# Two interleaved memory-transformer layers: Q, K and V in 128-row chunks with row-tiled tails, PSUM in single banks, W2 summed over two units

## The chip, the cores and the metric

The kernel runs on one core of one Trainium2 chip. The metric is the device time of one execution in microseconds, here as the median of 3 runs. TensorE (PE) multiplies, VectorE (DVE) and ScalarE (ACT) move results out of PSUM and do the elementwise work, GpSimd (POOL) does one small operation a normalization, and SyncE (SP) issues the loads of weights.

## The reference

Two blocks alternate, twice: a segment-recurrent attention A and a gated feed-forward B, each on the normalized input and with a residual.

```python
x = x + A(layernorm(x)); x = x + B(layernorm(x))
x = x + A(layernorm(x)); x = x + B(layernorm(x))   # the same weights both times
# A: S = 2048 in 64 segments of 32 rows, 8 memory rows, D = 576, 32 heads of 128
for s in range(64):
    h = concatenate([mem, x[32*s:32*s+32]])         # 40 rows
    q, k, v = h @ Wq, h @ Wk, h @ Wv                # each 576 -> 32 x 128
    p = softmax(where(mask, q @ k.T * 128**-0.5, -1e9))
    o = (p @ v) @ Wo                                # back to 576
    mem, out[s] = o[:8], o[8:]
# B: silu(x @ w1) * (x @ w3) @ w2, with 576 -> 4608 -> 576
```

All inputs and the output are bf16. A segment needs the memory that the segment before it left, so the 64 segments of a layer follow each other.

## The kernel before

The two layers run interleaved: at step t layer 0 works on segment t and layer 1 on segment t - 8 (`LAG = 8`), so 56 of the 72 steps hold both layers (80 columns) and the first and last eight hold one (40). Every four steps a job runs the FFN for one block of 128 rows of each layer; it is spread over the next four steps. It goes by 18 units (`NPR`) of 256 of the 4608 columns; a unit's w1, w3 and w2 are loaded anew for each job.

What runs in which order is decided before the program is built. `make_nodes` describes the work as nodes, each with an engine, an assumed duration, dependencies, a priority and the buffer slots that it takes and gives back. `plan` walks through them like a list scheduler, and the instructions are emitted in the order that comes out, which every engine's queue keeps. A node with the engine "AD" goes to ScalarE or VectorE, whichever is free first.

The steps of attention, by the names in the trace: QK (for 8 units of 4 heads, Q and K of those heads into PSUM, then copied to `QKT`), VX and VM (V of the segment's rows and of the memory rows, copied to the tiles `VX` and `VM`), and then for 4 groups of 8 heads: SC (scores into `SB`), softmax on VectorE with the exponential on ScalarE (`SME`, `STAT`, `PB`), TR (transposes of `PB`, copied to `PTS`), PV (copied to `OT`) and WO (summed in `YB` over all groups). At the end of a step the new memory is copied from `YB` into the columns of the next step's `HT`, the transposed normalized input ("Ymem"). In the FFN, FF is the product with w1 and w3 in one, `HTT` its gated activation, and W2 the way back, which VectorE adds to the residual `XR`.

D = 576 is 9 chunks of 64 rows. `HT` and `XTB` hold every chunk twice, once in each half of the 128 partitions, and the weights hold Wq (w1) in the upper half and Wk (w3) in the lower one, so that two 64-row matmuls run at a time. V's weights lie the same way, by heads, and V's outputs take column strips of 32, so that eight matmuls of 64 rows and 32 columns run at a time. The core of QK:

```python
for hl in range(4):
    for c in range(NCH):
        for r in (0, 1):
            rr = slice(r * R64, (r + 1) * R64)
            self.mm(self.pair(pair)[:, r, hl * 2 * QW + q0:hl * 2 * QW + q1], self.T.WQK[rr, c, h0:h0 + E],
                    HTt[rr, POS[c], q0:q1], c == 0, c == NCH - 1, tile_position=(r * R64, 0))
```

Each `mm` is a weight load and a matmul of its own. PSUM is 3 pairs of banks that all these products share, one bank for the scores and the transposed probabilities (`SB`), and one for `YB`. A pair comes free when both its halves have been copied out. Every instruction goes through a helper, so that in the profile all matmuls have line 467, VectorE's work line 473 and ScalarE's line 470; the tiles tell them apart.

Of the kernel before, what the change touches and what calls it, by code (L numbers as in the profile page):

```python
# [35 lines left out]
EW_LAT = 0.13  # L36
NOW = 1.0e18

# [8 lines left out]
class Node:  # L47
# [3 lines left out]
    def __init__(self, eng, dur, fn, deps=(), prio=0.0, mode=None, acq=(), rel=(), name="", lat=None):  # L51
# [4 lines left out]
        self.outs, self.ready, self.start, self.end, self.by = [], 0.0, None, None, None  # L56
        self.left = len(self.deps)


def plan(nodes, pools, mode_pen=0.12, hold=0.0):  # L60
# [29 lines left out]
    while done < len(nodes):  # L90
# [50 lines left out]
        for o in n.outs:  # L141
            lat = n.lat
            if o.eng == e and e in ("ACT", "DVE", "PE"):
# [10 lines left out]
def ew(n, psum=True):  # L154

    return (0.07 + n * 0.000833 if psum else 0.11 + n * 0.000833, 0.065 + n / 960.0)


def dve(n):
    return 0.065 + n / 960.0  # L160


def actc(n):
    return 0.07 + n * 0.000833


def make_nodes(em, nseg, dma_bw=230e3, load_bw=340e3):
# [4 lines left out]
    def node(*a, **k):  # L172
# [4 lines left out]
    pools = {"pair": 3, "s": 1, "y": 1, "qkt": 4, "vx0": 1, "vx1": 1, "vm": 1, "sme": 2, "pb0": 1, "pb1": 1, "pts": 1, "ot": 1,  # L177
             "xr": 4, "xn": 2, "w13": 2, "w2": 2, "htt": 2}
    nst = nseg + LAG

# [4 lines left out]
    def load(name, nbytes, prio, fn):  # L185
        return node("DMA", nbytes / load_bw, fn, prio=prio, name=name, lat=2.0)

    kb = lambda rows, cols: rows * cols * 2
    ld_x0, ld_m0 = None, None
# [3 lines left out]
    order = [("qk", 0), ("qk", 1), ("v", 0), ("v", 1), ("v", 4), ("v", 5), ("v", 2), ("v", 3), ("v", 6), ("v", 7),  # L193
             ("o", 0), ("qk", 2), ("qk", 3), ("o", 1), ("qk", 4), ("qk", 5), ("o", 2), ("qk", 6), ("qk", 7), ("o", 3)]
    for what, i in order:
# [3 lines left out]
        elif what == "v":  # L199
            ld_v[i] = load("ldv", kb(576, 512), pr, em.load_v(i))  # L200
        else:
            ld_o[i] = load("ldo", kb(1024, 576), pr, em.load_o(i))

    m0p = Slot("pair")
    m0t = node("PE", 0.3, em.m0_tr(m0p), deps=[ld_m0], prio=-5, mode="full", acq=[m0p], name="m0tr")
    m0e = node("DVE", 0.5, em.m0_ev(m0p), deps=[m0t], prio=-5, rel=[m0p], name="m0ev")

# [4 lines left out]
    stores = {}  # L212
# [3 lines left out]
    def ln_nodes(tag, src, xn, deps, prio, writers, wdeps):  # L216

        acq = [] if src is xn else [xn]
        a = node("DVE", 0.72 + 0.12 + 0.07, em.ln_stats(src, xn), deps=deps, prio=prio, acq=acq, name=tag + "stats")
        b = node("POOL", 0.45, em.ln_pow(xn), deps=[a], prio=prio, name=tag + "pow")  # L220
        c = node("DVE", 0.5, em.ln_norm(src, xn), deps=[b], prio=prio, name=tag + "norm")
        pair = Slot("pair", users=len(writers))
        d = node("PE", 5 * 0.056, em.ln_tr(xn, pair), deps=[c] + list(wdeps), prio=prio, mode="full", acq=[pair], rel=[xn],
                 name=tag + "tr")
        out = []
        for eng, n, fn in writers:
            cost = ew(n)
            out.append(node(eng, cost if eng == "AD" else (cost[0] if eng == "ACT" else cost[1]), fn(pair), deps=[d],
                            prio=prio, rel=[pair], name=tag + "wr"))
        return c, out  # L230

    def ht_writers(li, g):
        w = []
        for r in (0, 1):
            for half in (0, 1):
# [815 lines left out]
```

## Time and profile before

| | |
|---|---|
| Median of 3 runs | 3476.67 us (3463.12 to 3481.11) |
| The profiled execution: time, span of its instructions | 3458.9 us, 3456.9 us |
| PE busy | 2949.1 us (85%), 92853 matmuls |
| VectorE, ScalarE, GpSimd busy | 2242.8 us (65%), 1207.7 us (35%), 65.3 us (2%) |
| DMA | 327.62 MB, mean 95 GB/s |

Busy time is the union of an engine's instructions. A matmul's row begins when it starts and has a modelled end, and the next one can start long before that end, so that a mean of 199 ns for one matmul and a rate of many more than five a microsecond go together. Idle time is charged to what released the next instruction; "issue" is a wait for nothing that the profile shows.

### The profile page before, as it was taken

Reading aid. Unit: us, or ns where it says so; the run is one execution under the profiler, and the core shown is the slowest. Engines: PE = TensorE matmul, PEld = TensorE weight load, DVE = VectorE, ACT = ScalarE, POOL = GpSimd, SP = SyncE. Lnnn points to the kernel's source line nnn. Section 1 sums busy time; section 2 is a strip of 40 time slices with the busy share of each in tenths; the row PEclk is TensorE's granted clock in tenths of the full one; section 3 lists DMA queues with packets and bytes.
Section 4 is the critical chain, followed back from the end, with each engine's and each line's share of the span. In section 5 each row is a group of like instructions: output and inputs, shape, how many; then the busy total and the mean of one; then the engine's idle time right before and its main releaser. Section 6 shows DMA issues by size and latency. Waiting matters only on the chain.

```text
span 3456.9 us, 196772 instructions
## 1 busy us (share of the span) xinstructions
PE 2949.1 (85%) x92853; PEld 2414.3 (70%) x92853; DVE 2242.8 (65%) x4915; ACT 1207.7 (35%) x2607; POOL 65.3 (2%) x108
## 2 busy tenths in 40 slices
PE   3777888899888988889898988999888989888776
PEld 2566767777777777777777777777777777766664
DVE  2355657677666766676776766676766777666554
ACT  1233333343333334343433333343333334332221
POOL 0000000000000000000000000000000000000000
PEclk8789999999999999999999999999999999999898
DMA  9135444434343433434343443443343443444448
GB/s 223 28 71 107 91 106 91 96 80 92 76 108 77 97 90 81 96 82 92 80 101 80 98 92 75 96 100 78 79 98 80 102 89 80 96 91 96 94 107 192
DMA packets 485515, 327.62 MB, mean 95 GB/s; under 512 B 16344, under 2 KB 482144, under 8 KB 484704
## 3 DMA queue, kind: packets, MB, share of 16 engines
q1 hardware_dynamic: 481632, 307.96, 40.3%
q8 instruction: 725, 11.88, 1.5%
q0 software_dynamic: 3072, 7.08, 0.7%
q14 instruction: 86, 0.70, 0.1%
HBM read 310.26 MB, written 2.36 MB: 90 GB/s over the span
## 4 chain that ended last, share of the span: by engine, by line
PE 63%; DVE 17%; issue 11%; ACT 5%; SPq 2%; DMA 1%; POOL 0%; POOLq 0%; ACTq 0%; DVEq 0%
PE pair L467 51%; PE YB L467 7%; PE SB L467 5%; DVE HTT L473 4%; DVE STAT L473 3%; DVE PB L473 3%; DVE SME L473 3%; SPq L476 2%; DVE XR L473 1%; ACT HT L470 1%; ACT SME L470 1%; DMA W<-in_B_w_dram 1%; DVE VX L473 1%; DVE HT L473 1%; DVE LNS L473 1%
## 5 line engine op out<-in xcount | busy, mean ns | idle before, releaser
L467 PE MATMUL pair<-HT,WQK 64*128 64x80 bf16 (+1 forms) x41472 | 812.7, 195 | 265.9 <-issue 226.1
L467 PEld LDWEIGHTS <-WQK 64*128 64x128 bf16 x42048 | 771.6, 97 | 337.2 <-issue 307.2
L467 PE MATMUL pair<-XTB,W 64*128 64x256 bf16 (+1 forms) x11016 | 610.0, 262 | 30.2 <-issue 11.4
L467 PEld LDWEIGHTS <-W 64*128 64x128 bf16 x11016 | 505.1, 95 | 89.5 <-issue 44.8
L470 ACT ACTIVATE QKT<-pair 128x320 bf16<-128x320 f32 (+1 forms) x790 | 301.4, 407 | 735.9 <-PE pair L467 703.2
L467 PE MATMUL pair<-WV,HT 64*32 64x512 bf16 (+1 forms) x14400 | 453.0, 390 | 52.8 <-DVE HT L473 15.4
L467 PE MATMUL YB<-OT,WO 128*128 128x80 bf16 (+1 forms) x11520 | 443.4, 198 | 21.0 <-issue 11.6
L467 PEld LDWEIGHTS <-WO 128*128 128x128 bf16 x11520 | 417.6, 100 | 45.0 <-issue 39.0
L473 DVE SCALAR_TENSOR_TENSOR XR<-pair,XR 128x576 f32<-128x576 f32 x576 | 416.9, 752 | 27.2 <-PE pair L467 17.9
L473 DVE CAST QKT<-pair 128x320 bf16<-128x320 f32 (+1 forms) x362 | 164.5, 455 | 384.7 <-ACT QKT L470 367.5
L467 PEld LDWEIGHTS <-HT 64*32 64x32 bf16 (+1 forms) x14400 | 203.1, 92 | 245.5 <-issue 86.3
L467 PE MATMUL pair<-W2C,HTT 128*128 128x288 bf16 x2232 | 347.9, 290 | 21.3 <-DVE HTT L473 12.5
L473 DVE SCALAR_TENSOR_TENSOR HTT<-HTT,pair 128x512 bf16<-128x512 bf16 (+1 forms) x324 | 202.1, 624 | 214.2 <-ACT HTT L470 210.9
L473 DVE TENSOR_TENSOR PB<-SME,STAT 40x256 bf16<-40x256 f32 (+1 forms) x1024 | 321.9, 319 | 20.5
L470 ACT ACTIVATE HTT<-pair 128x512 bf16<-128x512 f32 (+1 forms) x324 | 177.4, 547 | 445.3 <-PE pair L467 443.9
L473 DVE TENSOR_REDUCE STAT<-SME 104x8 f32<-104x320 f32 (+1 forms) x576 | 277.8, 482 | 80.8 <-ACT SME L470 67.1
L467 PEld LDWEIGHTS <-HTT 128*128 128x128 bf16 x2304 | 201.6, 99 | 105.0 <-issue 37.9
L470 ACT ACTIVATE OT<-pair 128x640 bf16<-128x640 f32 (+1 forms) x255 | 163.7, 642 | 237.8 <-PE pair L467 229.4
L470 ACT ACTIVATE SME<-SME 104x320 f32<-104x320 f32 (+1 forms) x288 | 134.7, 468 | 270.8 <-DVE SME L473 269.8
L473 DVE CAST VX<-pair 128x512 bf16<-128x512 f32 x128 | 88.5, 692 | 210.6 <-ACT VX L470 210.6
L473 DVE TENSOR_TENSOR HTT<-HTT,pair 128x512 bf16<-128x512 bf16 (+1 forms) x324 | 203.3, 628 | 11.2
L467 PE MATMUL SB<-ident,PB 104*128 104x104 bf16 x2304 | 162.1, 215 | 33.0 <-DVE PB L473 13.2
(66 smaller groups left out, 2039.3 us busy)
## 6 DMA issues: line engine op xcount, KB each, us to landing
W<-in_B_w_dram SPq DMA_DIRECT2D x612, 288.0 KB, 4.9
W2C<-in_B_w_dram SPq DMA_DIRECT2D x306, 288.0 KB, 3.9
WQK<-in_B_w_dram SPq DMA_DIRECT2D x16, 576.0 KB, 14.5
WQK<-in_A_Wq_dram SPq DMA_DIRECT2D x8, 576.0 KB, 15.1
WQK<-in_A_Wk_dram SPq DMA_DIRECT2D x8, 576.0 KB, 15.1
WV<-in_A_Wv_dram SPq DMA_DIRECT2D x8, 576.0 KB, 16.1
XR<-in_A_x_dram POOLq DMA_DIRECT2D x16, 288.0 KB, 3.4
WO<-in_A_Wo_dram SPq DMA_DIRECT2D x4, 1152.0 KB, 18.1
```

The costliest lines, as they stand in the source:

```text
L467: self.ch("PE", self.nc.tensor.matmul(out, lhsT=lhsT, rhs=rhs, start=start, stop=stop, skip_group_check=True, **k))
L470: self.ch("ACT", self.nc.scalar.activation(*a, **k))
L473: self.ch("DVE", getattr(self.nc.vector, fn_)(*a, **k))
L476: self.ch("SP", self.nc.sync.dma_start(out=out, in_=in_))
```

## The change

Q, K and V use four chunks of 128 rows and one tail of 64 (4 x 128 + 64 = 576). The four whole chunks go over the full height of the array; the tails go as 64-row tiles, Q's tail in one half of the array and K's in the other, or for V the tails of two head groups. Main part and tail are two nodes that add into the same bank, and the planner may put other work between them. `HT` holds the four chunks once and only the tail twice, so that its writes are one copy of 128 partitions and two small ones; the memory's write-back at the end of a step is three copies on ScalarE (two on each engine before). Weights are loaded in the new layout, and Q, K and V in slightly other pieces and order.

PSUM is six single banks in place of three pairs; a product that needs two takes two, each is given back by its own copy, and a product that needs one takes one. `OT` is copied in two pieces for this reason. The FFN's W2 waits for two units and sums both in PSUM, so that VectorE adds to `XR` half as often, in two pieces of 288 columns. There are 3 buffers for w2 and 4 for `HTT` (2 and 2). The planner's priorities and assumed durations have new numbers. FF itself keeps its nine chunks of 64 rows (`ff_split` is off).

```diff
+POOLS = {"bank": 6, "s": 1, "y": 1, "qkt": 4, "vx0": 1, "vx1": 1, "vm": 1, "sme": 2, "pb0": 1, "pb1": 1, "pts": 1, "ot": 1,
+         "xr": 4, "xn": 2, "w13": 2, "w2": 3, "htt": 4}
...
-    pools = {"pair": 3, "s": 1, "y": 1, "qkt": 4, "vx0": 1, "vx1": 1, "vm": 1, "sme": 2, "pb0": 1, "pb1": 1, "pts": 1, "ot": 1,
-             "xr": 4, "xn": 2, "w13": 2, "w2": 2, "htt": 2}
...
             for u in (2 * g, 2 * g + 1):
                 q = Slot("qkt", users=1)
-                pair = Slot("pair", users=2)
-                n = node("PE", 36 * mm80, em.qk(t, u, q, pair), deps=hx + hm + ([ld_qk[u]] if t == 0 else []),
-                         prio=t + 0.05 + 0.02 * u, mode="row", acq=[q, pair], name="QK")
-                rd.append(n)
+                b = banks()
+                pq = t + o.qk + o.ustep * u
+                m_ = node("PE", 32 * mm80, em.qk(t, u, b), deps=hx + hm[:1] + ([ld_qk[u]] if t == 0 else []),
+                          prio=pq, mode="full", acq=[q] + b, name="QK")
+                n = node("PE", 4 * mm80, em.qk_tail(t, u, b), deps=[m_] + hm[1:], prio=pq + o.qkt, mode="row", name="QKt")
+                rd += [m_, n]
...
             for (bi, g) in ents:
-                pair = Slot("pair")
-                d = node("PE", 4 * 0.1225, em.ffn_down(bi, pr_, htt, w2, pair, last), deps=[b] + (ld if last else [ld2]), prio=prio + 0.1,
-                         mode="full", acq=[pair], rel=[htt] + ([w2] if w2 else []), name="W2")
-                e_ = node("DVE", dve(576), em.ffn_add(g, xr[g], pair), deps=[d], prio=prio + 0.1, rel=[pair], name="W2a")
-                w2_last[bi] = e_
+                b = banks()
+                d = node("PE", 8 * 0.1225, em.ffn_down(bi, pp, htts, w2s, b, last), deps=mids + lds, prio=prio + o.w2,
+                         mode="full", acq=b, rel=htts + w2s, name="W2")
+                es = [node("DVE", dve(288), em.ffn_add(g, h, xr[g], b[h]), deps=[d], prio=prio + o.w2, rel=[b[h]], name="W2a")
+                      for h in (0, 1)]
+                w2_last[bi] = es
...
+    def v_mm(self, t, b, strips, tail):
+
+        HTt = self.ht(t)
+        W = self.wv(tail)
+        for c in ((4,) if tail else range(4)):
+            for r in (0, 1):
+                for p0, c0, c1, q in strips:
+                    out = self.bk(b[r])[p0:p0 + c1 - c0, :]
+                    if tail:
+                        rr = slice(r * R64, (r + 1) * R64)
+                        self.mm(out, HTt[rr, 4, c0:c1], W[rr, q * 512:(q + 1) * 512], False, True, tile_position=(r * R64, p0))
+                    else:
+                        w0 = (4 * r + q) * 512
+                        self.mm(out, HTt[:, c, c0:c1], W[:, c, w0:w0 + 512], c == 0, False, tile_position=(0, p0))
...
-    def qk(self, t, u, q, pair):
+    def qk(self, t, u, b):
+
         def f(n):
             q0, q1 = self.qcols(t)
             HTt = self.ht(t)
             for hl in range(4):
                 h0 = (4 * u + hl) * E
-                for c in range(NCH):
-                    for r in (0, 1):
-                        rr = slice(r * R64, (r + 1) * R64)
-                        self.mm(self.pair(pair)[:, r, hl * 2 * QW + q0:hl * 2 * QW + q1], self.T.WQK[rr, c, h0:h0 + E],
-                                HTt[rr, POS[c], q0:q1], c == 0, c == NCH - 1, tile_position=(r * R64, 0))
-        return f
...
+                for kind in (0, 1):
+                    for c in range(4):
+                        self.mm(self.bk(b[kind])[:, hl * 2 * QW + q0:hl * 2 * QW + q1], self.T.W[:, 4 * kind + c, h0:h0 + E],
+                                HTt[:, c, q0:q1], hl == 0 and c == 0, False)
+        return f
+
+    def qk_tail(self, t, u, b):
         def f(n):
             q0, q1 = self.qcols(t)
...
+            HTt = self.ht(t)
+            for hl in range(4):
+                h0 = (4 * u + hl) * E
+                for kind in (0, 1):
+                    rr = slice(kind * R64, (kind + 1) * R64)
+                    self.mm(self.bk(b[kind])[:, hl * 2 * QW + q0:hl * 2 * QW + q1], self.T.W[rr, 8, h0:h0 + E],
+                            HTt[rr, 4, q0:q1], False, hl == 3, tile_position=(kind * R64, 0))
+        return f
...
+            for half in range(2):
+                for i in range(2):
+                    W = self.tail_w[2 * pp + i][1] if last else self.T.W2C[:, w2s[i].i]
+                    for fb in range(2):
+                        self.mm(self.bk(b[half])[:, 0:288], self.T.HTT[:, htts[i].i, fb, bi * P:(bi + 1) * P],
+                                W[:, fb, half * 288:(half + 1) * 288], i == 0 and fb == 0, i == 1 and fb == 1)
```

In the built program PE's matmuls go from 92853 to 68021, and each still has a weight load of its own. The order shows the change on three engines.

PE, at the start of a step in the middle of the program, where a W2 of the FFN gives way to Q and K; before, the matmuls of a unit go to the two halves of one pair, and 72 of them stand in a row.

```order
L467 LDWEIGHTS HTT_87
L467 MATMUL pair1_89<-W2C_86,HTT_87 128x288
L467 LDWEIGHTS WQK_64
L467 MATMUL pair0_88<-HT_70,WQK_64 128x80
L467 LDWEIGHTS WQK_64
```

The same place after: a unit's 32 whole-height matmuls stand ahead of this W2, four in a row for each of the banks 4 and 1, and its eight tails behind it, alternating between the two banks.

```order
L478 LDWEIGHTS HTT_87
L478 MATMUL bank5_93<-W2C_86,HTT_87 128x288
L478 LDWEIGHTS W_64
L478 MATMUL bank4_92<-HT_70,W_64 128x80
L478 LDWEIGHTS W_64
L478 MATMUL bank1_89<-HT_70,W_64 128x80
```

What moved: a unit of Q and K is split around other work, and its tail is a block of its own in another tiling.

VectorE, at the end of a job: the additions of W2 to the residual `XR` and the normalization that follows them, before.

```order
L473 SCALAR_TENSOR_TENSOR HTT_87<-HTT_87,pair2_90 128x512
L473 TENSOR_TENSOR HTT_87<-HTT_87,pair2_90 128x512
L473 SCALAR_TENSOR_TENSOR XR_72<-pair1_89,XR_72 128x576
L473 SCALAR_TENSOR_TENSOR XR_72<-pair0_88,XR_72 128x576
L473 SCALAR_TENSOR_TENSOR XR_72<-pair1_89,XR_72 128x576
L473 BN_STATS LNS_75<-XR_72 128x6 x2
L473 BN_AGGR LNS_75<-LNS_75 128x2
```

The same place after.

```order
L484 CAST OT_83<-bank4_92 128x320
L484 SCALAR_TENSOR_TENSOR XR_72<-bank3_91,XR_72 128x288
L484 SCALAR_TENSOR_TENSOR XR_72<-bank5_93,XR_72 128x288
L484 BN_STATS LNS_75<-XR_72 128x6 x2
L484 BN_AGGR LNS_75<-LNS_75 128x2
L484 TENSOR_SCALAR LNS_75<-LNS_75 128x1
L484 SCALAR_TENSOR_TENSOR XR_72<-bank0_88,XR_72 128x288
L484 SCALAR_TENSOR_TENSOR XR_72<-bank2_90,XR_72 128x288
```

What moved: two units now share one addition, made of two pieces with a bank each, and half of an `OT` copy stands on VectorE.

ScalarE, at the end of a step, where the new memory goes from `YB` to `HT`, before.

```order
L470 ACTIVATE VX_77<-pair1_89 128x512
L470 ACTIVATE OT_83<-pair0_88 128x640
L470 ACTIVATE HTT_87<-pair2_90 128x512
L470 ACTIVATE HT_70<-YB_91 64x4x16 x2
L470 ACTIVATE YTS_84<-YB_91 128x5x32 x2
```

The same place on ScalarE after.

```order
L481 ACTIVATE OT_83<-bank3_91 128x320
L481 ACTIVATE VX_77<-bank0_88 128x512
L481 ACTIVATE HT_70<-YB_94 128x4x16
L481 ACTIVATE HT_70<-YB_94 64x16 x2
L481 ACTIVATE VX_77<-bank4_92 128x512
L481 ACTIVATE YTS_84<-YB_94 128x5x32 x2
```

What moved: the memory's copies are all on ScalarE, one over 128 partitions and two small ones for the tail.

## Rows read from the trace of the kernel before

**Rows 1.** The page's span and busy times of the engines.

```profile
span 3456.9 us, 196772 instructions
PE 2949.1 (85%) x92853; PEld 2414.3 (70%) x92853; DVE 2242.8 (65%) x4915; ACT 1207.7 (35%) x2607; POOL 65.3 (2%) x108
```

**Rows 2.** The page's DMA queues, PE's instructions: packets, MB, share of 16 engines.

```profile
q8 instruction: 725, 11.88, 1.5%
```

**Rows 3.** PE's waits over the span: what for, us in total, times, longest.

```profile
PE pair L467 <- issue: 263.0, 229, 4.7
PE pair L467 <- DVE HTT L473: 27.3, 70, 1.0
PE SB L467 <- issue: 21.6, 21, 4.3
...
PE YB L467 <- issue: 11.6, 18, 2.1
PE pair L467 <- DVE VX L473: 11.1, 31, 0.4
```

**Rows 4.** Timeline, PE, 1703 to 1711 us: start, us, what, count [idle before].

```profile
1703.46 1.93 PE L467 MATMUL pair<-HT,WQK 64*128 64x80 bf16 x98 [0.34 <-issue]
...
1706.93 1.40 PE L467 MATMUL pair<-HT,WQK 64*128 64x80 bf16 x68 [0.24 <-issue]
...
1708.25 0.43 PE L467 MATMUL SB<-QKT 128*64 128x40 bf16 x16
...
1708.61 0.96 PE L467 MATMUL pair<-HT,WQK 64*128 64x80 bf16 x44
...
1710.40 0.68 PE L467 MATMUL pair<-HT,WQK 64*128 64x80 bf16 x28 [0.82 <-issue]
```

**Rows 5.** Timeline, PE, 1713 to 1716 us.

```profile
1713.45 1.46 PE L467 MATMUL pair<-HT,WQK 64*128 64x80 bf16 x72
...
1714.96 0.20 PE L467 MATMUL pair<-PTS,VX 64*128 64x80 bf16 x2
...
1715.00 0.20 PE L467 MATMUL pair<-PTS,VM 64*128 64x80 bf16 x2
...
1715.13 0.43 PE L467 MATMUL SB<-QKT 128*64 128x40 bf16 x16
```

**Rows 6.** Timeline, PE, 1737 to 1742 us.

```profile
1737.15 1.61 PE L467 MATMUL YB<-OT,WO 128*128 128x80 bf16 x40
1738.69 2.14 PE L467 MATMUL pair<-WV,HT 64*32 64x512 bf16 x72
```

**Rows 7.** Groups of instructions by shape: count | busy us, mean ns | idle before, releasers.

```profile
L467 PE MATMUL pair<-HT,WQK 64*128 64x80 bf16 x32256 | 665.2, 199 | 177.1 <-issue 157.9 <-DVE VM L473 11.2 <-DVE HTT L473 6.7
L473 DVE SCALAR_TENSOR_TENSOR XR<-pair,XR 128x576 f32<-128x576 f32 x576 | 416.9, 752 | 27.2 <-PE pair L467 17.9
L473 DVE SCALAR_TENSOR_TENSOR HTT<-HTT,pair 128x512 bf16<-128x512 bf16 x252 | 171.9, 682 | 161.6 <-ACT HTT L470 159.0
L467 PE MATMUL pair<-HT,WQK 64*128 64x40 bf16 x9216 | 147.5, 180 | 88.9 <-issue 68.2 <-DMA WQK<-in_A_Wk_dram 10.3 <-ACT HT L470 5.4
L467 PE MATMUL YB<-OT,WO 128*128 128x40 bf16 x2560 | 81.5, 185 | 11.1 <-issue 7.0 <-ACT OT L470 3.9
L473 DVE SCALAR_TENSOR_TENSOR HTT<-HTT,pair 128x256 bf16<-128x256 bf16 x72 | 30.1, 418 | 52.6 <-ACT HTT L470 52.0
L470 ACT ACTIVATE HT<-YB 64x64 bf16<-64x64 f32 x110 | 23.8, 216 | 51.4 <-PE YB L467 42.2 <-DVE HT L473 8.7
```

**Rows 8.** PE's waits from 3300 us to the end.

```profile
PE pair L467 <- issue: 19.6, 16, 3.3
...
PE pair L467 <- DMA WQK<-in_B_w_dram: 2.5, 2, 2.2
```

**Rows 9.** Busy us of each engine in a stretch, granted clock, DMA share, GB/s.

```profile
86.00:432.00 346.00, 272.31 (x10313) 221.17 (x10314) 184.61 (x477) 109.35 (x287) 4.95 (x8) 0.88 0.35 74
```

More of the change, by code (lines that the diff above doesn't have):

```diff
@@ L56, in __init__, with after @@
         self.outs, self.ready, self.start, self.end, self.by = [], 0.0, None, None, None
+        self.left = len(self.deps)
+    def after(self, *more):
+        for d in more:
+            if d is not None:
+                self.deps.append(d)
         self.left = len(self.deps)
@@ L151, in plan, with actc, dve, dveh @@
     return order, idle
[L154 to L167, printed above, removed]
+def actc(*ns):
+    return sum(0.067 + n * 0.000833 for n in ns)
+def dve(*ns):
+    return sum(0.065 + n / 960.0 for n in ns)
+def dveh(*ns):
+    return sum(0.065 + n / 1920.0 for n in ns)
+def ew(*ns):
+    return (actc(*ns), dve(*ns))
+def ewh(*ns):
+    return (actc(*ns), dveh(*ns))
+class Opt:
+    qk, qkt, sc, tr, pv, wo, wog = 0.0372, -0.0358, 0.0268, 0.0346, 0.0, 0.3, 0.049
+    vm, vmt, vx, vxt = 0.1, 0.0813, 0.55, 0.102
+    ff, fft, win, w2 = 0.2124, -0.05, 3.6429, -0.0064
+    gstep, ustep = 0.005, 0.02
+    mode_pen, hold = 0.12, 0.0
+    ff_split = False
+def make_nodes(em, nseg, pools, o=Opt, dma_bw=230e3, load_bw=340e3):
     ngrp = nseg // 4
@@ L175, in node, with banks, load @@
         return n
-    pools = {"pair": 3, "s": 1, "y": 1, "qkt": 4, "vx0": 1, "vx1": 1, "vm": 1, "sme": 2, "pb0": 1, "pb1": 1, "pts": 1, "ot": 1,
-             "xr": 4, "xn": 2, "w13": 2, "w2": 2, "htt": 2}
+    def banks(n=2):
+        return [Slot("bank") for _ in range(n)]
     nst = nseg + LAG
+    kb = lambda rows, cols: rows * cols * 2
     def layers_of(t):
         return [li for li in (0, 1) if 0 <= t - LAG * li < nseg]
[L185 to L189, printed above, removed]
+    def load(name, nbytes, prio, fn, deps=()):
+        return node("DMA", nbytes / load_bw, fn, deps=deps, prio=prio, name=name, lat=2.0)
     ld_m0 = load("m0", kb(8, D), -10, em.load_m0())
@@ L485, in cp, with bk, bk_bf @@
             self.v("tensor_copy", out, in_)
-    def pair(self, s):
-        return self.T.pairs[s.i]
-    def pair_bf(self, s, n):
-        return self.pair(s)[:, 0, :].bitcast(BF)[:, 0:n]
+    def bk(self, s):
+        return self.T.banks[s.i]
+    def bk_bf(self, s, n):
+        return self.bk(s)[:].bitcast(BF)[:, 0:n]
     def layers(self, t):
@@ L794, in pt_ev, with pv @@
         return f
-    def pv(self, t, g, pts, pair):
+    def pv(self, t, g, pts, b):
         def f(n):
@@ L830, in wo, with y_mem @@
         return f
-    def y_mem(self, t, nxt, r, half):
+    def y_mem(self, t, nxt, tail):
         def f(n):
@@ L869, in span, with ffn_up @@
         return min(bis) * P, (max(bis) + 1) * P
-    def ffn_up(self, ents, pr, w13, pair, last):
+    def ffn_up(self, ents, pr, w13, b, last):
         def f(n):
@@ L989 @@
     T.M0 = T.XTB[:].rearrange("p a b -> p (a b)")[:, 0:D]
-    T.pairs = [pp.tile([P, 2, 512], F32, name=f"pair{i}") for i in range(pools["pair"])]
+    T.banks = [pp.tile([P, 512], F32, name=f"bank{i}") for i in range(pools["bank"])]
     T.YB = pp.tile([P, 512], F32, name="YB")
@@ L1009 @@
     nc.vector.memset(T.SB[:], 0.0)
-    for p in T.pairs:
-        nc.vector.memset(p[:], 0.0)
-    order, _ = plan(nodes, pools)
+    for b in T.banks:
+        nc.vector.memset(b[:], 0.0)
+    order, _ = plan(nodes, pools, Opt.mode_pen, Opt.hold)
     for n in order:
```

426 lines of the change are left out of this document (203 added, 223 removed).

## The prediction

> **What bounds the kernel now.** I read the page's first part, then TensorE's waits, then the timeline at the places where the waits lie. TensorE (PE) is busy 2949.1 of 3456.9 us, VectorE 65%, ScalarE 35% [rows 1], so PE's order of work sets the time and 507.8 us of it stand idle. The waits say what for [rows 3]: 263.0 + 21.6 + 11.6 = 296.2 us in 229 + 21 + 18 = 268 waits are "issue", in which nothing that the profile shows was waited for. The other 211.6 us have a name (a copy, a softmax step, a weight load); the longest of them is the gated activation HTT with 27.3 us.
>
> The timeline shows what the issue waits are [rows 4]. PE pauses before 1703.46, 1706.93 and 1710.40 us: three pauses 3.47 us apart. From the second to the third it ran 68 + 16 + 44 = 128 matmuls, each with a weight load of its own: 256 instructions. The queue of PE's instructions brought 725 packets, 11.88 MB [rows 2], so 16 KB a packet. PE has 2 x 92853 instructions [rows 1], and 185706 / 725 is again 256. So PE stands still at the end of each packet, because the next one has not come: where it is short, a packet comes every 3.47 us.
>
> Q and K eat a packet faster than that. Without a pause, 72 of their 64-row matmuls take 1.46 us [rows 5]. A row's last matmul is drawn 0.199 us long [rows 7], so they follow each other every (1.46 - 0.20) / 71 = 17.7 ns, and 128 take 2.3 us. The 64-row pairs run side by side: 35.4 ns a pair is the time of 80 columns at 2.4 GHz (33.3 ns). The array itself is not badly used; it is the instructions that run out.
>
> The drawn end hides a part of each pause, since the next matmul could have started 0.018 us after the last one's start, not 0.199. So a wait is 0.18 us longer than written: 296.2 + 268 x 0.18 = 344 us of pauses.
>
> **The change, term by term.**
>
> *Q and K.* 72 matmuls a unit become 32 with 128 rows and 8 in the 64-row tiling. The array's time stays: 32 + 8/2 = 36 slots as before 72/2 = 36. What a 128-row slot costs is seen at WO: 40 in 1.61 us, (1.61 - 0.20) / 39 = 36 ns [rows 6], weight load for every matmul included, against 35.4. With 40 columns (one layer alive, the first and last eight steps) WO takes (81.5 + 11.1) / 2560 = 36 ns and a 64-row pair, its issue waits of 68.2 off, (147.5 + 88.9 - 68.2) / 4608 = 36.5 [rows 7]. No gain and no loss in the array. But 128 matmuls now last 4.6 us, over the 3.47 us of a packet. V: 72 matmuls in 2.14 us today are nine rounds of eight, 0.213 us each [rows 6]; after, eight rounds of four and one of eight, the same nine rounds, 54 ns a matmul instead of 27, so a packet lasts 6.9 us instead of 3.4.
>
> *Pauses.* PE's matmuls fall from 92853 to 68021 in the built order, packets to 531. What stays faster than a packet are scores, PV and the tails, in runs of 8 to 32. Bounds for what remains of 344 us: nothing below; above, the rate at which WO pauses today, though it stands among Q and K: 11.6 + 18 x 0.18 = 14.8 us in 11520 / 128 = 90 packets, 0.165 us each, 88 us for 531. I take 35, nearer to the low end because WO inherits its shortage from Q and K in front of it. In the last 157 us 19.6 us of the issue waits [rows 8] lie where PE also waits for the last weights to load; I count 15 of them as not won. Term: **-294 us** (-241 to -344).
>
> *Mode changes.* A tail in a tiling of its own makes PE change tiling. Price, from [rows 5]: PV matmuls start 0.035 us apart (two by two), the first score 0.13 us after the last PV pair: 0.095 us more. From WO to V it is 1738.69 - (1737.15 + 39 x 0.036) = 0.136, 0.10 more than a step [rows 6]. Changes of tile shape in the built order: 1547 before, 1962 after. 415 x 0.097 = **+40 us** (0 if they fall where PE waits anyway; 83 at twice the price). The Trainium skill speaks against this part: its page "TensorEngine Tiling (Array Packing)", section Key Properties, says that a change of tiling mode drains the array. The trace agrees, at 0.095 us each. The page gives no price. The Trainium skill's page "TensorE: Matmul & The Clock Gate", section Step-by-step, tells of a drain of some 128 cycles, by which I estimate 0.053 us a change, 22 us in all, and a sum 18 us lower.
>
> *W2 over two units.* The 2304 matmuls stay; they come as eight to a block of rows, after both units' HTT. Half as many places wait for HTT: (27.3 + 70 x 0.18) / 2 = **-20 us** (0 to -40) [rows 3]. VectorE's additions become 576 of 288 columns for 576 of 576. At 256 and 512 columns such an operation takes 418 and 682 ns [rows 7], so 451 at 288: 576 x (752 - 451) = 173 us of VectorE's time. That is nothing on the path while VectorE is 65% busy; part of it is taken back by copies of OT, 220 half-size ones on VectorE in the built order for 33 whole ones.
>
> *At nothing.* Single banks: each is freed by its own copy, where the pair waited for both copies one after the other; PE's wait for the second of the VX copies, 11.1 us in all [rows 3], shows what that costs now. The memory's write-back is three ScalarE copies for four on two engines; with its cover (FFN matmuls that PE has in hand) gone, it costs at most a copy of 0.216 us [rows 7] in each of 72 steps, 16 us. Start-up loads move the same bytes.
>
> Sum: 3456.9 - 294 + 40 - 20 = 3183 us of span, 3185 with the 2 us around it, against the profiled 3458.9. The median of the runs shown, 3476.67, is 0.5% above that execution, so the forecast is 3185 x 1.005 = **3200 us**.
>
> **Rivals.**
>
> *Pauses come by the packet, not by the rate.* If each packet costs its mean whatever PE does in it, 344 x 531 / 725 = 252 us stay and 92 go: 3457 - 92 + 40 - 20 = 3385, as a median 3404. For: every long pause lies at a packet's end. Against: the pauses sit in Q and K (157.9 + 68.2 of the 296.2 us, [rows 7]), with 45% of the matmuls; WO's packets pause 0.165 us each, the mean packet 344 / 725 = 0.47. Chance 0.10.
>
> *The other engines become the bound.* The pauses gave VectorE and ScalarE time. Without them a step is 8% shorter for 31 us of VectorE work in it (65% of 48). If the named waits grow by 150 us, seven tenths of today's 211.6, 3183 + 150 = 3333, as a median 3352. For: most named waits on PE are for a VectorE result [rows 3]. Against: VectorE loses work, and two thirds busy leaves room. Chance 0.12.
>
> *V's column strips don't overlap with 128 rows: slower.* Place: the 200 groups of V. Side by side in today's trace are eight 64-row tiles; four strips of 128 rows stand in no row. If they ran one after the other, 32 x 0.213 = 6.8 us would stand where eight rounds take 1.7, 5.1 us x 200 = 1020 us, and the kernel would take some 4200 us. It decides from 274 / 200 = 1.4 us a group on, strips overlapping less than half. Against: four column strips do run side by side today, in each row half. Chance 0.04.
>
> *More than forecast.* From 86 to 432 us the granted clock was 0.88 [rows 9], so some 83 of 346 us ran at 1.2 GHz, in a stretch with pauses. If PE keeps 2.4 GHz there and the named waits shrink too, 3060 is possible. Chance 0.06.
>
> **How the numbers follow.** The forecast's case has 0.68; its own range is 3110 to 3290 (terms at their ends, not all at once). The range that should hold 8 in 10 takes in half of the second rival and reaches up toward the first: 3085 to 3340. A change of 0.5% (17 us) is about what a measurement of this kernel can tell from none. All cases but V's end faster by more; I give 0.93 faster, 0.02 within 0.5%, 0.05 slower, the last two for V and for mishaps of dependencies past 250 us.
>
> **What would show it.** PE's issue waits at 20 to 90 us instead of 296; 531 packets of instructions, 8.7 MB; a unit's 32 matmuls of Q and K 36 ns apart, with no pause at each 128th; a V group still near 2 us; waits for HTT halved; VectorE's addition at 450 ns; PE busy above 90% of the span. The prediction is wrong if the issue waits stay above 150 us (the packet rival), if waits with names pass 300 us (the engines), or if V's group takes over 3 us.

## The result, and the profile after

The changed kernel takes 2977.95 us (median of 4 runs, 2975.72 to 2985.86) against 3476.41 us before (4 runs): a ratio of 0.8576 [0.8547, 0.8604], 498 us less. The forecast was 3200 us with a range of 3085 to 3340. The direction was right; the gain was 1.8 times the forecast.

The page's span, busy times and PE's instruction queue:

```profile
span 2976.9 us, 147413 instructions
PE 2866.2 (96%) x68021; PEld 2342.9 (79%) x68021; DVE 2068.5 (69%) x5015; ACT 1078.2 (36%) x2684; POOL 63.7 (2%) x108
q8 instruction: 531, 8.70, 1.3%
```

PE's waits (what for: us in total, times, longest us):

```profile
PE bank L478 <- issue: 15.5, 18, 2.5
PE bank L478 <- DMA W<-in_B_w_dram: 10.9, 10, 3.1
PE YB L478 <- issue: 8.2, 5, 3.8
...
PE SB L478 <- DVE QKT L484: 7.7, 29, 0.3
...
PE bank L478 <- DVE HTT L484: 3.3, 6, 1.1
...
PE SB L478 <- issue: 2.4, 4, 1.6
```

The reader sees the pauses gone: issue waits are 15.5 + 8.2 + 2.4 = 26.1 us in 27 waits, where [rows 3] had 296.2 in 268. But PE's idle time fell by more than that, from 507.8 to 2976.9 - 2866.2 = 110.7 us. So the rest of the idle time (waits with a name, and gaps too short to be listed) fell too, from 211.6 to 110.7 - 26.1 = 84.6 us. Of that fall of 127 us the forecast had 20. The span's 480 us are thus 270 of issue waits, 127 of named waits and 83 of busy time. Each wait that is gone takes its drawn end of 0.18 us with it: 241 issue waits fewer are 43 us of busy time, and 187 listed waits with a name fewer (300 before, 113 now) are 34. The 415 new changes of tile shape add 37 (e7 below has their price). That leaves some 43 us of busy time without an account so far; the clock, taken up below beside the prediction's other terms, is worth about as much.

The timeline of PE at the start of a step (start, us, what, count), which answers to [rows 4, 5]:

```profile
1702.11 2.46 PE L478 MATMUL bank<-HT,W 128*128 128x80 bf16 x64
1704.39 1.23 PE L478 MATMUL bank<-W2C,HTT 128*128 128x288 bf16 x8
1705.55 0.46 PE L478 MATMUL bank<-HT,W 64*128 64x80 bf16 x16
1705.94 1.15 PE L478 MATMUL bank<-W2C,HTT 128*128 128x288 bf16 x8
1706.93 2.46 PE L478 MATMUL bank<-HT,W 128*128 128x80 bf16 x64
...
1734.64 3.64 PE L478 MATMUL bank<-WV,HT 128*32 128x512 bf16 x64
```

No row shows idle time before it. Q and K's whole-height matmuls start (2.46 - 0.20) / 63 = 35.9 ns apart, the tails (0.46 - 0.20) / 15 = 17.3 ns. V's 64 come in sixteen rounds of four; with a drawn end of 0.38 us the rounds start (3.64 - 0.38) / 15 = 0.217 us apart, 54 ns a matmul. The forecast had 36, 17.7 and 54.

Two groups by shape (count | busy us, mean ns | idle before):

```profile
L478 PE MATMUL bank<-HT,W 128*128 128x80 bf16 x14336 | 564.0, 202 | 2.0 <-ACT QKT L481 0.9 <-DVE HT L484 0.9
L484 DVE SCALAR_TENSOR_TENSOR XR<-bank,XR 128x288 f32<-128x288 f32 x576 | 246.9, 450 | 68.6 <-PE bank L478 61.7
```

Q and K had 157.9 us of issue waits ahead of them in [rows 7]; here 2.0 us in all. The addition to `XR` takes 450 ns (451 worked out).

The first two stretches of the span, the second of which answers to [rows 9] (busy us and count of each engine, granted clock, DMA share, GB/s; the share is the packets' time over that of 16 engines and can pass 1):

```profile
0.00:86.00 86.00, 52.15 (x1230) 38.64 (x1231) 35.56 (x98) 17.80 (x51) 5.14 (x15) 0.80 0.88 252
86.00:432.00 346.00, 325.62 (x9177) 267.49 (x9174) 222.49 (x598) 135.06 (x384) 6.83 (x11) 0.99 0.45 99
```

The granted clock from 86 to 432 us is 0.99 where it was 0.88; the first 86 us come back in e8.

### The profile page after: what moved, and what is told of

The parts are those of the page before. It is cut to its first block, busy times and chain, and to the rows that moved or that the text cites. A ratio compares the mean times of both kernels' runs of the same rounds, so it can differ in the third digit from the quotient of the medians.

```text
span 2976.9 us, 147413 instructions
## 1 busy us (share of the span) xinstructions
PE 2866.2 (96%) x68021; PEld 2342.9 (79%) x68021; DVE 2068.5 (69%) x5015; ACT 1078.2 (36%) x2684; POOL 63.7 (2%) x108
## 4 chain that ended last, share of the span: by engine, by line
PE 90%; issue 3%; DMA 3%; DVE 2%; ACT 1%; SPq 1%; POOLq 0%; POOL 0%; DVEq 0%; ACTq 0%
PE bank L478 70%; PE YB L478 13%; PE SB L478 7%; DMA W<-in_B_w_dram 1%; DMA W<-in_A_Wk_dram 1%; ACT HT L481 1%; SPq L487 1%; DVE QKT L484 1%; DVE SME L484 0%; DVE STAT L484 0%; ACT QKT L481 0%; DVE PB L484 0%; DVE HT L484 0%; DVE HTT L484 0%; ACT XTB L481 0%
## 5 line engine op out<-in xcount | busy, mean ns | idle before, releaser
L478 PEld LDWEIGHTS <-W 128*128 128x128 bf16 (+1 forms) x34632 | 1241.4, 97 | 163.3 <-issue 71.2
L478 PE MATMUL bank<-HT,W 128*128 128x80 bf16 (+3 forms) x23040 | 807.6, 197 | 13.9 <-issue 5.5
L478 PE MATMUL bank<-XTB,W 64*128 64x256 bf16 (+1 forms) x11592 | 621.4, 260 | 21.4 <-DMA W<-in_B_w_dram 10.9
L481 ACT ACTIVATE QKT<-bank 128x320 bf16<-128x320 f32 (+1 forms) x801 | 279.7, 408 | 591.7 <-PE bank L478 589.2
L478 PE MATMUL bank<-WV,HT 128*32 128x512 bf16 (+3 forms) x8000 | 457.8, 386 | 11.2 <-DMA WV<-in_A_Wv_dram 5.4
L481 ACT ACTIVATE HTT<-bank 128x512 bf16<-128x512 f32 (+1 forms) x324 | 178.1, 550 | 434.9 <-PE bank L478 432.7
L478 PE MATMUL bank<-W2C,HTT 128*128 128x288 bf16 x2232 | 321.8, 287 | 0.6 <-DVE HTT L484 0.2
L484 DVE SCALAR_TENSOR_TENSOR XR<-bank,XR 128x288 f32<-128x288 f32 x576 | 246.9, 450 | 68.6 <-PE bank L478 61.7
L484 DVE SCALAR_TENSOR_TENSOR HTT<-HTT,bank 128x512 bf16<-128x512 bf16 (+1 forms) x324 | 202.1, 624 | 126.1 <-ACT HTT L481 122.0
L484 DVE TENSOR_TENSOR HTT<-HTT,bank 128x512 bf16<-128x512 bf16 (+1 forms) x324 | 203.6, 628 | 24.5 <-DVE HTT L484 0.5
## 6 DMA issues: line engine op xcount, KB each, us to landing
WV<-in_B_w_dram SPq DMA_DIRECT2D x8, 576.0 KB, 15.5
```

Source lines behind the costliest of these rows:

```text
L478: self.ch("PE", self.nc.tensor.matmul(out, lhsT=lhsT, rhs=rhs, start=start, stop=stop, skip_group_check=True, **k))
L481: self.ch("ACT", self.nc.scalar.activation(*a, **k))
L484: self.ch("DVE", getattr(self.nc.vector, fn_)(*a, **k))
```

## The experiments

The theory after the result: the pauses went as forecast, and what the forecast missed came from the parts that decide the order of work (priorities, banks, buffers, W2 in twos) and from the loads. The rivals: the chunks brought it all, since pauses also made other waits; or the pauses were not a matter of matmul rate. The planner's assumed durations and the order of the loads stay new in every run that starts from the changed kernel, e10 too; no run prices them. Times are medians of 4 runs. The kernel before ran beside them in each set, with medians of 3471.55, 3455.07 and 3474.80 us in the three sets, so the ratios are the better measure across sets. Where a difference in us and one in ratios disagree, both are given.

### Is it the rate at which instructions come?

**e1.** The changed kernel, each of Q and K's main matmuls cut into two column halves that run side by side:

```diff
-    self.mm(self.bk(b[kind])[:, ...], self.T.W[:, 4 * kind + c, h0:h0 + E], HTt[:, c, q0:q1], ...)
+    for p0 in (0, R64):
+        self.mm(self.bk(b[kind])[p0:p0 + R64, ...], self.T.W[:, 4 * kind + c, h0 + p0:h0 + p0 + R64],
+                HTt[:, c, q0:q1], ..., tile_position=(0, p0))
```

> The changed kernel, but each 128-row matmul of Q and K is cut into two column halves of 64 that run side by side: 86453 matmuls for 68021, the same order, 23 more changes of tile shape, and the array's time as it was if the halves overlap. Rate theory (pauses come because Q and K use up instructions faster than a packet comes): the main matmuls start some 18 ns apart again, issue waits go from 26 back to 200 to 300 us, and the time from 2978 to 3230 to 3350 us. Plan theory (order, buffers and W2 gave the gain): at most 3020 us. If the halves do not overlap at all, 18432 more slots of some 25 ns each would add 460 us with few issue waits.

Measured: 3290.24 us, ratio 0.9491 [0.9462, 0.952], 312 us slower than the changed kernel (318 by ratios). PE's waits in e1, and two rows of its timeline:

```profile
PE bank L478 <- issue: 198.3, 183, 4.0
PE SB L478 <- issue: 16.4, 19, 2.1
PE YB L478 <- issue: 13.6, 13, 4.1
```

```profile
1702.80 2.43 PE L478 MATMUL bank<-HT,W 128*64 128x80 bf16 x125
1706.28 0.20 PE L478 MATMUL bank<-HT,W 128*64 128x80 bf16 x1 [1.05 <-issue]
```

The halves start (2.43 - 0.20) / 124 = 18.0 ns apart, so where both layers are alive the array does the same work in the same time, and the pauses are back: 228.3 us in 215 waits. What runs short there is instructions, not PE's array. In the sixteen steps with one layer it is not quite the same work: halves of 40 columns start 16 ns apart near the end of e1, 32 ns for both, and whole-height matmuls of 40 columns 25.5 ns in the changed kernel. By that, 4096 x 6.5 ns = 27 us of the 312 are array time (an estimate).

**e2.** The kernel before with K's matmuls left out (K's half of each bank keeps old values): `for r in (0,):` in place of `(0, 1)`.

> The kernel before, with K's matmuls left out (K's half of each bank keeps old values): 72117 matmuls for 92853, each remaining Q matmul alone in its half of the array, so the same array time of 36 slots a unit, same order, same buffers. Rate theory: the matmuls of Q are 35 ns apart, issue waits fall from 296 to 30 to 70 us, and the time from 3476 to 3100 to 3190 us; lower still if the named waits (212 us) were an effect of the pauses. Packet theory: 563 packets of the 725 keep 230 us of issue waits, 3390 us. Plan theory: 3430 us or more.

Measured: 3232.54 us, ratio 0.932 [0.9303, 0.9337]. PE's waits in e2:

```profile
PE pair L467 <- DVE HTT L473: 29.4, 74, 0.8
PE SB L467 <- DVE SME L473: 21.9, 46, 0.8
PE pair L467 <- issue: 20.6, 25, 2.0
...
PE YB L467 <- issue: 3.3, 5, 0.9
...
PE SB L467 <- issue: 1.2, 1, 1.2
```

The issue waits are 25.1 us, as the rate theory had it, but the time is 40 us above its range. Span less busy time is 3229.8 - 2942.6 = 287.2 us, so the waits with names are 262.1 us, 50 more than before: a first sign that without the pauses this kernel waits for other things instead, copies and weight loads among them.

### The parts of the change, each taken out

**e3**, priorities of before (1910 changes of tile shape in the built order for 1962):

```diff
-    qk, qkt, sc, tr, pv, wo, wog = 0.0372, -0.0358, 0.0268, 0.0346, 0.0, 0.3, 0.049
-    vm, vmt, vx, vxt = 0.1, 0.0813, 0.55, 0.102
-    ff, fft, win, w2 = 0.2124, -0.05, 3.6429, -0.0064
+    qk, qkt, sc, tr, pv, wo, wog = 0.05, 0.0, 0.0, 0.0, 0.0, 0.3, 0.02
+    vm, vmt, vx, vxt = 0.1, 0.0, 0.55, 0.0
+    ff, fft, win, w2 = 0.0, -0.05, 3.75, 0.1
```

> The changed kernel with the priorities of the kernel before (Q and K by 0.02 a unit from t + 0.05, WO by 0.02, FFN over 3.75 of 4 steps, W2 0.1 behind it, tails at their main part's priority). 1910 changes of tile shape for 1962. Plan theory: the new numbers gave the fall of the named waits from 212 to 85 us, so that they come back and the time is 3080 to 3130 us. Rate theory: issue waits stay under 50 us and the time within 2960 to 3020 us.

Measured: 3055.82 us, ratio 0.8807 [0.8794, 0.8821], 78 us slower. The planner's numbers alone are a part of the gain that no term of the forecast held. Issue waits stay under 20 us; PE is idle 3054.8 - 2885.1 = 169.7 us in place of 110.7.

**e4**, W2 for each unit by itself, so that `XR` gets 1152 additions of 288 columns:

```diff
-    for i in range(2):
-        for fb in range(2):
-            self.mm(self.bk(b[half])[:, 0:288], self.T.HTT[:, htts[i].i, fb, ...], ..., i == 0 and fb == 0, i == 1 and fb == 1)
+    for fb in range(2):
+        self.mm(self.bk(b[half])[:, 0:288], self.T.HTT[:, htt.i, fb, ...], ..., fb == 0, fb == 1)
```

> The changed kernel with W2 by single units again, each added to the residual in two pieces of 288 columns: 1152 additions of 450 ns, 259 us more of VectorE's busy time (69% to about 77%), buffers as in the changed kernel. If W2 over two units was worth its predicted 20 us: 2990 to 3010 us. If VectorE's relief is what made the named waits fall: waits for HTT and softmax results back to 60 us or more, 3040 to 3100 us.

Measured: 3008.77 us, ratio 0.8671 [0.8656, 0.8687], 31 us slower (33 by ratios), above the 20 us of the forecast and inside its range. VectorE is busy 2216.7 us for 2068.5, 148 more and not the 259 expected, since the planner moved some copies to ScalarE (1121.9 us for 1078.2). By drawn times e4's additions take 1152 x 0.450 = 518 us, those of the kernel before 417 [rows 7], so that e4 may price this step too high.

**e5**, PSUM as three pairs again:

```diff
-POOLS = {"bank": 6, ...
+POOLS = {"bank": 3, ...
...
-        return [Slot("bank") for _ in range(n)]
+        s = Slot("bank", users=n)
+        return [Half(s, i) for i in range(n)]
...
-    T.banks = [pp.tile([P, 512], F32, name=f"bank{i}") for i in range(pools["bank"])]
+    T.banks = [pp.tile([P, 2, 512], F32, name=f"bank{i}") for i in range(pools["bank"])]
```

> The changed kernel with PSUM as three pairs again: both banks of a pair are taken together and come free when both copies are done; everything else stays (1974 changes of tile shape in the built order, 1962 in the changed kernel). Theory 1, single banks were a part of why the named waits fell from 211.6 to 84.6 us: waits with names grow by 20 to 60 us and the time is 3000 to 3040 us. Theory 2, as the prediction had it, single banks are worth nothing on the path: 2970 to 2990 us.

Measured: 3047.37 us, ratio 0.8818 [0.8798, 0.8838], 69 us slower (84 by ratios), more than either theory gave. Its largest PE waits:

```profile
PE bank L486 <- DVE QKT L492: 31.1, 41, 0.9
PE SB L486 <- DVE QKT L492: 18.9, 30, 0.6
PE bank L486 <- DVE VX L492: 14.6, 29, 1.0
```

Two rows on the tile QKT in e5, from two lists, what was waited for and who waited (us, times):

```profile
  ACT QKT L489: 175.9, 131
...
  DVE QKT L492: 167.8, 99
```

ScalarE's copies of QKT were waited for, and nearly all of that by VectorE's: with a pair, VectorE's copy of one half starts only when ScalarE's copy of the other has ended. The same place of the program in e5, and then in the changed kernel, with what PE waits for behind it:

```profile
1706.09 1.09 ACT L489 ACTIVATE QKT<-bank 128x320 bf16<-128x320 f32 x3 [4.01 <-PE bank L486]
1706.56 1.28 DVE L492 CAST QKT<-bank 128x320 bf16<-128x320 f32 x3 [3.34 <-ACT QKT L489]
1707.10 0.37 PE L486 MATMUL SB<-QKT 128*64 128x40 bf16 x14 [0.63 <-DVE QKT L492]
```

```profile
1664.53 1.10 ACT L481 ACTIVATE QKT<-bank 128x320 bf16<-128x320 f32 x3 [4.01 <-PE bank L478]
1664.63 1.29 DVE L484 CAST QKT<-bank 128x320 bf16<-128x320 f32 x3 [3.33 <-PE bank L478]
1665.18 0.37 PE L478 MATMUL SB<-QKT 128*64 128x40 bf16 x14 [0.26 <-DVE QKT L484]
```

With pairs VectorE starts 0.47 us behind ScalarE and is released by ScalarE's copy; with single banks it starts 0.10 us behind and is released by PE. PE's scores behind them wait 0.63 us and 0.26.

The trace of the kernel before had it in rows that the prediction did not read: who waited for the copies of QKT, and, in the list of another tile, for those of VX.

```profile
  DVE QKT L473: 367.5, 245
...
  DVE VX L473: 210.6, 127
```

Not all of that is the pair's price: a wait is put down to what ended it, and of the 3.34 us in the window of e5 the pair adds some 0.37 (0.47 less 0.10). In the changed kernel's lists for these two tiles no copy of VectorE's waits for one of ScalarE's.

**e7**, every tail right behind its main part (2447 changes of tile shape):

```diff
-    qk, qkt, ... = 0.0372, -0.0358, ...
-    vm, vmt, vx, vxt = 0.1, 0.0813, 0.55, 0.102
+    qk, qkt, ... = 0.0372, -90.0, ...
+    vm, vmt, vx, vxt = 0.1, -90.0, 0.55, -90.0
```

> The changed kernel with every tail given the priority to stand right behind its main part: 2447 changes of tile shape instead of 1962, the same matmuls. Theory 1, a change costs 0.095 to 0.1 us on the path wherever it stands: 485 x 0.097 = +47 us, 3010 to 3040 us. Theory 2, changes lie in time in which TensorE waits anyway: 2970 to 2990 us. Theory 3, other work between main part and tail is also cover for copies that the next blocks wait for: over 3050 us, and the named waits grow by more than 30 us.

Measured: 3016.07 us, ratio 0.8725 [0.87, 0.8751], 38 us slower (52 by ratios). PE's busy time in e7:

```profile
PE 2909.8 (97%) x68021; PEld 2364.9 (79%) x68021; DVE 2050.4 (68%) x4869; ACT 1150.8 (38%) x2830; POOL 63.6 (2%) x108
```

It is 43.6 us more for the same matmuls, and idle time falls a little (102.1 us for 110.7). A change of tile shape costs 43.6 / 485 = 0.090 us of PE's time (0.078 to 0.107 by the times). The Trainium skill's page "TensorEngine Tiling (Array Packing)", section Key Properties, has it that a change of mode drains the array; e7 agrees, and stands at the 0.095 read from [rows 5] rather than at the 0.053 that the prediction estimated from the Trainium skill's page "TensorE: Matmul & The Clock Gate", section Step-by-step.

**e8**, the weights of Q, K and V in pieces of 64 partitions:

```diff
-    self.dma(self.T.W[:, 4 * kind:4 * kind + 4, c0:c1], wd[0:4 * P, c0:c1].rearrange("(c p) n -> p c n", p=P))
+    src = wd[0:4 * P, c0:c1].rearrange("(c p) n -> p c n", p=P)
+    for r in (0, R64):
+        self.dma(self.T.W[r:r + R64, 4 * kind:4 * kind + 4, c0:c1], src[r:r + R64])
...
```

> The changed kernel with the weight loads of Q, K and V issued in pieces of 64 partitions as before, twice as many, the same bytes. Theory 1, the first step ended some 34 us earlier (before: 100.8 us, after: 66.9 us) because pieces of 128 partitions land faster: TensorE is busy about 30 of the first 86 us instead of 52, and the time is 3000 to 3015 us. Theory 2, it came from the order of the loads and of the first step's work: the first 86 us stay as they are and the time is 2970 to 2985 us.

Measured: 2997.24 us, ratio 0.867 [0.8647, 0.8693], 19 us slower (33 by ratios). The first 86 us of e8, and then of the kernel before:

```profile
0.00:86.00 86.00, 34.65 (x678) 24.57 (x682) 23.59 (x61) 10.79 (x26) 4.57 (x14) 0.79 1.08 237
```

```profile
0.00:86.00 86.00, 30.43 (x875) 21.53 (x875) 20.34 (x49) 9.80 (x21) 6.18 (x14) 0.80 1.08 223
```

PE is busy 34.65 us of them, 30.43 before and 52.15 in the changed kernel, so most of the earlier start comes from the pieces' shape; the time lies just under theory 1's range or in it, by which measure one takes. The loads of Wq, as issues (KB each, median us to landing), of the changed kernel:

```profile
W<-in_A_Wq_dram SPq DMA_DIRECT2D x8, 512.0 KB, 8.1
```

and of the kernel before:

```profile
WQK<-in_A_Wq_dram SPq DMA_DIRECT2D x8, 576.0 KB, 15.1
```

### The chunks alone, and parts put back

**e10.** Taken together, e3, e4, e5 and two buffers each for w2 and `HTT`: what stays of the change are the chunks with tails, the loads, the copies' shapes and the additions of 288 columns. The diffs are those above, with

```diff
-         "xr": 4, "xn": 2, "w13": 2, "w2": 3, "htt": 4}
+         "xr": 4, "xn": 2, "w13": 2, "w2": 2, "htt": 2}
```

> The changed kernel with everything undone that orders work rather than shapes matmuls: the old priorities, PSUM in pairs, W2 for each unit by itself (1152 additions of 288 columns), two buffers each for w2 and HTT; what stays are chunks of 128 rows with tails, the same 68021 matmuls (2005 changes of tile shape). Theory 1, the forecast had the chunks right and failed at what it priced at nothing: 3110 to 3200 us, with named waits of 150 us or more and issue waits under 40 us. Theory 2, the chunks bring nearly all of it by themselves: 3050 to 3100 us. Theory 3, the parts need each other (slower than the sum of the single experiments): over 3200 us.

Measured: 3264.51 us, ratio 0.9444 [0.9422, 0.9466]. Its page and PE's largest waits:

```profile
span 3265.8 us, 147865 instructions
PE 2940.3 (90%) x68021; PEld 2374.0 (73%) x68021; DVE 2223.2 (68%) x5452; ACT 1188.7 (36%) x2820; POOL 60.0 (2%) x108
```

```profile
PE bank L484 <- DVE QKT L490: 48.6, 65, 1.1
PE bank L484 <- DVE HTT L490: 46.3, 65, 1.2
PE bank L484 <- DVE VX L490: 26.4, 60, 1.0
PE SB L484 <- DVE PB L490: 22.4, 46, 3.3
PE bank L484 <- ACT HT L487: 19.0, 29, 2.0
```

The issue waits are gone (8.3 us), and PE is idle 325.5 us all the same: 317 us of waits with names, 106 more than before, most of them for copies. Theory 3 held in its number: the single experiments cost 178 us together (78, 69 and 31), and all of it undone costs 286.

**e11, e12, e13** put one part back each (single banks; the new priorities; the buffers), and **e14** is e4 with two buffers each. The diffs are the above, turned round.

> The chunks alone (3264.5 us, ratio 0.944) with one part of the change added: six single banks in place of three pairs (1963 changes of tile shape). Taking single banks out of the changed kernel cost 69 us (ratio 0.858 to 0.882). Theory 1, the parts add up: ratio 0.915 to 0.925, 3165 to 3195 us. Theory 2, the parts need each other, and what one frees another one holds up: ratio 0.93 or more, over 3220 us. Theory 3, each part by itself takes away most of the same waits: ratio under 0.905, under 3130 us.

> The chunks alone (3264.5 us, ratio 0.944) with the new priorities added, all else as there (1970 changes of tile shape). Taking the new priorities out of the changed kernel cost 78 us (ratio 0.858 to 0.881). Theory 1, the parts add up: ratio 0.915 to 0.928, 3165 to 3205 us. Theory 2, the parts need each other: ratio 0.935 or more, over 3230 us. Theory 3, each part by itself takes away most of the same waits: ratio under 0.905, under 3130 us.

> The chunks alone (3264.5 us, ratio 0.944) with three buffers for w2 and four for HTT (two and two), all else as there (1985 changes of tile shape). The waits for HTT are 46.3 us in 65 there. Theory 1, the buffers are the part that is still unexplained: the three parts taken out one by one cost 78 + 69 + 31 = 178 us of the 286 between the chunks alone and the changed kernel, the other 108 are the buffers: ratio 0.91 to 0.92, 3150 to 3180 us. Theory 2, the buffers only take most of the HTT waits: ratio 0.930 to 0.938, 3215 to 3240 us, HTT waits under 15 us. Theory 3, nothing: within 10 us of the chunks alone.

> The changed kernel with W2 for each unit by itself (3008.8 us, ratio 0.867) and with two buffers each for w2 and HTT as before, single banks and new priorities kept (1950 changes of tile shape). Theory 1, the buffers are worth the 108 us that the three other parts do not explain: 3100 us or more, ratio 0.893 or more. Theory 2, they are worth 20 to 50 us: ratio 0.873 to 0.882. Theory 3, nothing with the new priorities: ratio 0.865 to 0.870, and what is missing between the chunks alone and the changed kernel is that the parts help each other.

Measured: e11 3149.33 us, 0.9066 [0.9046, 0.9086]; e12 3115.96, 0.8967 [0.8944, 0.899]; e13 3273.17, 0.9418 [0.9389, 0.9447]; e14 3008.39, 0.8662 [0.8642, 0.8682]. With W2 by unit the buffers are worth nothing, with the old priorities (e13) or the new ones (e14). No run has W2 over two units with two buffers each, where it takes two of `HTT` at a time. e13's HTT waits stay at 46.9 us in 67, so HTT was late by itself and not for want of a buffer. e11 lies between theories 1 and 3, and for e12 theory 3 held.

The runs also show where the 108 us are that the three single experiments left over. Banks and priorities nearly add up: 115 and 149 us by themselves, 256 together (e10 to e14; by ratios 131, 166 and 272). What makes up for part of either is W2 over two units. Beside both it is worth 31 us (e4), beside the priorities alone 69 (e12 to e5), beside the banks alone 94 (e11 to e3; by ratios 33, 52 and 90), the buffers counted as nothing. So each of banks and priorities costs less when it is taken out of a kernel that has W2 over two units. In e11 the largest of PE's waits is one for the additions to `XR`:

```profile
PE bank L476 <- DVE XR L482: 31.8, 49, 2.0
```

In e3, with W2 over two units, it is 0.5 us.

In a row, each adding one part to the one above it:

| | us | difference | by ratios x 3476 |
|---|---|---|---|
| before | 3476 | | |
| e10: chunks, tails, loads, copies' shapes | 3264.5 | -212 | -193 |
| e12: with the new priorities | 3116.0 | -149 | -166 |
| e14: with single banks | 3008.4 | -108 | -106 |
| e4: with three and four buffers | 3008.8 | 0 | +3 |
| changed kernel: W2 over two units | 2978.0 | -31 | -33 |

Each row of this table holds for its place: W2 over two units would bring more further up. And crossed, with issue waits and named waits of PE (the idle time less the issue waits):

| | old order of work | new order of work |
|---|---|---|
| short matmuls of Q and K | before: 3476 us; 296 and 212 us | e1: 3290 us; 228 and 78 us |
| chunks | e10: 3264 us; 8 and 317 us | changed: 2978 us; 26 and 85 us |

One half alone brings 186 to 212 us (177 to 193 by ratios), both 498: some 100 us are there only when both are done. The cross is not a clean one. The new loads (e8), V's chunks and the copies' shapes stand in both halves and are counted twice, and e1 has matmuls of its own that are some 27 us slower; so the 100 is rough. The chunks alone meet the copies, the new order alone meets the pauses.

## Why the prediction was wrong in its size

**Pauses, right.** The term was -294 us of 344, 50 to stay. By the same measure 26.1 + 27 x 0.18 = 31 us stay, and e1 shows that the rate of instructions makes them. The packet rival (252 us to stay) is refuted by the 26 us. Packets came out at 531.

**Mode changes, right.** The forecast had 415 x 0.097 = 40 us; at e7's 0.090 it is 37. V's strips overlap, 54 ns a matmul, so the slower rival is out. One reading under "Q and K" was wrong and did no harm: with 40 columns the prediction had 36 ns from sums that hold drawn ends and other idle time; rows near the end of the kernel before show 25, for WO (under "The clock") and for a 64-row pair, so that "no gain and no loss in the array" stands.

**W2 over two units, right in size by luck.** The term was -20 us (0 to -40), for half as many places that wait for HTT; e4 measures 31 to 33. HTT is little of it: its waits are 7.7 us in e4 and 3.3 in the changed kernel, where the kernel before had 27.3, so most of their fall came from the rest of the order. The other waits that grow in e4 are for ScalarE's copies of VX (1.5 to 9.3 us) and for FFN weights (10.9 to 17.4). What the term put at nothing was the time that VectorE saves: beside banks or priorities alone the step is worth 52 to 94 us.

**Single banks "at nothing", the step that failed.** The prediction said that a pair waited for both copies one after the other and took PE's wait for the second VX copy, 11.1 us [rows 3], as the price. It looked at PE's wait alone, in the old order. The second copy's own wait stood in VectorE's rows, 367.5 + 210.6 us for QKT and VX, with what it would have waited for anyway. PE's waits for VectorE's copies of QKT and VX were 13.7 us before, and 14.2 in e2, where the pauses are gone and the old order stays. With the chunks and pairs they are 89.3 us (e10) and 64.6 (e5), in the changed kernel 7.9. So what a pair costs depends on the order around it, and 11.1 us did not carry over; why PE meets these copies in the one order and not in the other is not shown. Single banks are worth 69 to 131 us, depending on what else is done (e5 at the low end in us, e10 to e11 at the high end by ratios).

**The order of work, left out.** The priorities stand in the change, and no term of the sum is for them; they are worth 78 us taken out of the changed kernel (e3) and 149 to 166 added to the chunks alone (e12). That is the other step that failed, a term put at nothing without a reason.

**"Other engines become the bound", the rival at 0.12.** Its mechanism is real: e10 shows it, with named waits up by 106 us of the 150 it assumed (50 in e2, where the pauses went with K's matmuls and the order stayed). In the whole change it did not come, because banks, priorities and W2 took 232 of those 317 us away. So the forecast erred twice, in opposite ways: without the W2 term its sum gives some 3220 us for the chunks, and e10, with the faster loads in it, takes 3264; the parts at nothing then bring 286. The prediction held the named waits fixed in its own case and let them rise in the rival; it had no case in which the parts beside the chunks took them down, beyond the mention of shrinking waits at 0.06.

**Start-up loads "move the same bytes", wrong.** The bytes are the same and the landings are not; e8 gives 19 to 33 us.

**The clock, in no term but the rival at 0.06.** The granted clock from 86 to 432 us rose from 0.88 [rows 9] to 0.99, and over the whole span from 0.964 to 0.986. With levels of 1.2 and 2.4 GHz that is 249 us at the lower level before and 83 after. Two rows of the kernel before have the price, the first at a granted clock of 0.50, the second at 1.00:

```profile
3251.32 1.54 PE L467 MATMUL YB<-OT,WO 128*128 128x40 bf16 x40
...
3257.41 1.16 PE L467 MATMUL YB<-OT,WO 128*128 128x40 bf16 x40
```

The matmuls start (1.54 - 0.20) / 39 = 34 ns and (1.16 - 0.18) / 39 = 25 ns apart. At that price the 166 us that are no longer at the lower level are worth up to 166 x (1 - 25 / 34) = 44 us, less where PE stood idle in them. This is an estimate, of the size of the busy time left over above; no run changes the clock alone. Nor do the pauses alone set it: from 86 to 432 us it is 0.89 in e2, with the pauses gone, 0.95 in e1, with them back, and 0.96 in e10.

## What to carry to other kernels

When an engine's idle time has two causes of like size, price the removal of one with the other left in: here each half brought about 200 us and both 500. A part's worth depends on what else is done: W2 over two units was worth 31 us or 94, so one experiment that takes it out does not price it. Where two engines copy halves of one PSUM buffer, read in the copying engines' rows whether the second copy waits for the first; PE's rows show only what reaches PE in that order of work. A planner's new numbers in a diff are a change of their own and want a term, or at least a range.

## What the runs showed of the hardware

PE's instructions come in packets of 16 KB, 256 instructions, one in about 3.5 us where they are short [rows 4]; a weight load and a matmul every 18 ns need one in 2.3 us. In e1, with the array's work nearly unchanged, that cost 228 us of drawn waits. The Trainium skill's page "Runtime: NRT & Kernel Launch", section Instruction fetch mechanics, has the same blocks, and says that the cost of crossing into the next is "mostly hidden". The size agrees (8.70 MB / 531); that it is hidden holds in the changed kernel (26 us) and not in e1 or before (228 and 296 us).

Weights that go to 128 partitions in one transfer landed in 8.1 us for 512 KB, and in 15.1 us for 576 KB to 64 partitions; the first 86 us moved 252 against 223 GB/s, at a DMA share of 0.88 against 1.08. In e8 half the bytes a piece took 9.3 us in the median for Wq and 7.5 for Wk. A landing time is not a piece's alone, though: Wo's pieces, the same in all three, landed in 18.1 us before, 8.6 in the changed kernel and 9.0 in e8.

A change of the array's tile shape cost 0.090 us (e7, 485 more of them).
